# A new written-out order for a fused attention and mixer kernel, with other banks and tile shapes on TensorE

## The chip, the cores and the metric

The kernel runs on one core of one Trainium2 chip. The metric is the device time of one execution in microseconds (us). Before the change the median of three runs is 119.66 us (119.56 to 119.93). Beside the timed runs there is one profiled execution of 119.62 us, from which all rows of the trace come.

## The reference: what is computed

There are 8 batch items and 8 heads, with 576 rows of 64 elements each. Attention is taken twice. First 32 packed queries `p` attend to `k` and `v`. Then the 576 queries `q` attend to the 32 packed results. The result, 576 x 512 per item, goes through a token mixer with a ReLU and through an output projection.

```python
p_packed = sm_attn(p, k, v)                  # softmax over 576 keys
x = sm_attn(q, p_packed, p_packed)           # softmax over the 32 packed rows
wq, wk = x @ w_q, x @ w_k                    # 576 x 64 each, per item
W_tok = scale * (wq @ wk.T)                  # 576 x 576
out = relu(W_tok @ x) @ w_out                # 576 x 512
```

## The kernel before: tiles, engines and an order written by hand

There is no loop over items in the usual sense. A string named SCHEDULE (from line 10 on) lists every operation of all 8 items, each once, and line 742 calls them in that order. Each engine executes its own instructions in exactly the order in which the list names them; an instruction that has to wait holds up everything behind it on its engine. An entry has the form name@item, then the engine that executes it (v is VectorE or DVE, s is ScalarE or ACT, g is GpSimd or POOL), or, for TensorE (PE), the PSUM bank and a letter for the tile shape.

The operations of one item, in the order of its data:

- LK, LQ, LV load the keys, queries and values. POOL issues these loads on one queue, in the order of the list. Item 0's keys come by another way: in fp32 through SyncE (k_f, line 185), are cast by cA and cB, transposed by kf0 to kf3 and copied out of PSUM by kfe0 to kfe3. LP, tp, lp, tr and lq bring the packed queries into pT_bd.
- kt0 to kt2 and qt0 to qt2 transpose keys and queries on PE (line 306); ke and qe copy the result out of PSUM (lines 162 on ACT and 168 on DVE).
- s0 (line 327) multiplies the packed queries with the keys, nm (line 337, DVE) takes the row maximum, ex (line 343, ACT) the exponential, xt (line 155) transposes it, xe copies it out.
- pv (line 401) multiplies with the values. In an "E" form (line 391) it uses smaller tiles and 72 instead of 36 instructions. pp (line 418, DVE) scales, pt and pte transpose and copy out.
- et and em (lines 454 and 471) are the scores of the queries against the packed rows; mx, sb, x, sm, rr, ml (lines 483 to 527) are their softmax, on DVE, ACT and POOL. In items 0 and 7 it is cut into two parts. at and ae transpose and copy the result, a2T.
- pq, wk, wl, wq, g, y (lines 439 to 646) are the two projections and the mixer's inner products, with copies out pqe, wke, wqe, ge, ye. The mixer's own multiplication is m0, m1 and, for two items at once, m2 (lines 663 and 687), followed by the ReLU r.
- o0 to o4 (line 706) are the output projections, oe copies them out, st and sc store.
- u is a multiplication of zeros whose result nothing reads (line 213). It fills PE at the start.

PE's array is used in several tile shapes. Most operations exist with 128 x 64 tiles, two instructions side by side for the two halves of the output, and with letter A in the full 128 x 128 shape, with half as many instructions. pv and y use 64 x 64 tiles; m0 and m1 use 64 x 64, or with letter C 64 x 128.

Of the kernel before, what the change touches and what calls it, by code (L numbers as in the profile page):

```python
# [7 lines left out]


SCHEDULE = """  # L10
    LK@1 LP@0 LQ@0 cA1@0s u@0:0 u@0:0 u@0:0 u@0:0 u@0:0 u@0:0 u@0:0 u@0:0 u@0:0 tp@0:3 cA0@0s
# [1 line left out]
    kfe3@0s cw3@0 kfe0@0s u@0:1 u@0:1 u@0:1 s0@0:4 nm0@0 nm1@0 u@0:1 u@0:1 u@0:1 kt1@1:0 kt0@1:3
    ex0@0 ke1@1v cw2@0 kt2@1:1 ke0@1v ex1@0 tr@0:27 ke2@1s cw1@0 xt0@0:4A lq1@0v rc1@0 lq0@0v
    mk@0 u@0:0 u@0:0 u@0:0 u@0:0 u@0:0 qt0@0:5 xt1@0:1 qt2@0:3 cw0@0 xe1@0v qe2@0s xe0@0v s0@1:0
    qt1@0:6 nm0@1 u@0:7 u@0:7 pv@0:3 qe0@0v ex1@1 LK@3 pp0@0 qe1@0v ex0@1 u@0:7 u@0:7 pt@0:3
    pte@0v u@0:7 et@0:3 em@0 mx0@0 kt1@2:6 rc1@1 xt1@1:7 sb0@0 LQ@2 xt0@1:0A xe1@1s mx1@0
    kt0@2:1 x0@0 kt2@2:7 mk@1 sb1@0 ke2@2s ke0@2s ke1@2v x1@0 u@0:2 u@0:2 u@0:2 qt1@1:3 sm0@0v
    s0@2:4 qe1@1s rr0@0v xe0@1v ml0@0g sm1@0v u@0:2 u@0:2 qt2@1:0 qt0@1:2 qe2@1s nm0@2 LV@2
    at0@0:3A ae0@0s pv@1:0 rr1@0v ex0@2 pp0@1 ml2@0g qe0@1v u@0:7 u@0:7 pt@1:3A ml1@0g pq@0:0  # L20
    pte@1s ex1@2 et@1:1 em@1:A wo1@0 pqe@0s at1@0:4A mx0@1 xt0@2:0A wo0@0 ae1@0s pq@1:5 wk@0:7A
    wl@0 rc1@2 wq@0:4 sb0@1 wke@0s kt1@3:6 pqe@1s wkx@0g xt1@2:7A g@0:5A wqe@0v mk@2 x0@1
    kt2@3:1 ge@0v LK@4 kt0@3:2 y@0:3 xe0@2s sm0@1v qt2@2:5 LQ@3 ye@0s ke2@3s m0@0:34C ke0@3s
    LV@3 m1@0:01C r01@0s qt1@2:2 rr0@1v r00@0s xe1@2v ml1@1g ke1@3v qt0@2:7 qe2@2v qe0@2s pv@2:3
    ml2@1g r10@0v ml0@1g s0@3:5 pp0@2 r11@0s pt@2:3A qe1@2s nm0@3 at1@1:4A LQ@4 at0@1:0A pte@2s
    ae1@1s et@2:1 em@2:A ae0@1s LK@5 wk@1:0A ex0@3 mx0@2 wl@1 LV@4 o1@0:4 wke@1s ex1@3 o3@0:0
    wkx@1g sb0@2 LQ@5 g@1:5A pq@2:7 LK@7 ge@1s xt0@3:6 oe1@0v oe3@0s kt2@4:1 x0@2 kt1@4:5 LK@6
    ke2@4v kt0@4:0 o0@0:4 ke1@4s sm0@2v ke0@4s xt1@3:5 pqe@2s wq@1:2 y@1:0 rc1@3 wqe@1s qt2@3:7
    rr0@2v xe1@3v qt1@3:3 oe0@0s ml2@2g ye@1v qt0@3:2 ml1@2g qe1@3s qe2@3v m0@1:01C xe0@3s
    s0@4:3 r01@1s mk@3 m2@1:6 qe0@3s nm0@4 o2@0:7 r00@1s ml0@2g r2@1s pv@3:0 LV@5 ex1@4 o4@1:6A  # L30
    pp0@3 oe2@0v ex0@4 LQ@6 at0@2:0A pt@3:2A st1@0 at1@2:7A ae0@2s pte@3v m1@1:34C st0@0 ae1@2v
    et@3:0 r11@1s em@3:A oe4@1v r10@1s wk@2:7A rc1@4 mx0@3 xt1@4:5A xt0@4:6A xe1@4s qt2@4:3 wl@2
    qt0@4:5 wke@2s sb0@3 wq@2:4 qe2@4s wkx@2g o2@1:7 mk@4 x0@3 kt1@5:0 LV@6 kt2@5:1 ke1@5v
    qt1@4:2 qe0@4s pq@3:3 sm0@3v o3@1:0A wqe@2s qe1@4s g@2:4A ke2@5s xe0@4v o0@1:2A ge@2s pqe@3s
    rr0@3v oe3@1s ml1@3g y@2:3 oe0@1v pv@4:5 ye@2s m0@2:34 pp0@4 ml0@3g m1@2:20 r00@2s oe2@1v
    kt0@5:1 pt@4:5 r10@2s o1@1:6 r01@2v LQ@7 pte@4s r11@2s et@4:3 ml2@3g ke0@5s at0@3:7A em@4:A
    LV@7 ae0@3s o0@2:1A mx0@4 qt2@5:2 at1@3:7 qe2@5s sb0@4 o3@2:0 oe0@2s qt0@5:2 qt1@5:1 ae1@3v
    qe0@5s s0@5:3 oe1@1v x0@4 wk@3:2 qe1@5v wq@3:7 st0@1 nm0@5 kt2@7:6 st1@1 wqe@3s wl@3 o1@2:1
    ke2@7s wke@3v ex1@5 kt0@7:6 sm0@4v o2@2:7 wkx@3g ex0@5 kt0@6:2 oe3@2s g@3:3A rr0@4v oe1@2s
    xt1@5:4A ke0@6v ml2@4g xt0@5:5A ge@3s rc1@5 xe1@5v ml1@4g pq@4:2 kt1@6:1 pqe@4s y@3:3 xe0@5s  # L40
    ke1@6v kt2@6:2 ye@3s ml0@4g oe2@2s at1@4:5A ke2@6v m0@3:34C ke0@7s s0@6:0 ae1@4s mk@5 r01@3s
    pv@5:5 nm0@6 r00@3s at0@4:7A o1@3:3A ae0@4s pp0@5 ex0@6 wk@4:7A pt@5:5A ex1@6 m1@3:64C
    pte@5v wl@4 kt1@7:5 r11@3s wke@4v et@5:0 em@5:A oe1@3s rc1@6 wkx@4g o0@3:7A r10@3s mx0@5
    mk@6 ke1@7s g@4:4A qt0@6:5 sb0@5 wq@4:6 qe0@6s qt1@6:3 ge@4s wqe@4s o2@3:5 qe1@6s oe0@3v
    x0@5 s0@7:0 oe2@3v st0@3 m2@3:7A nm0@7 xt1@6:4A st0@2 r2@3s xt0@6:5A sm0@5g st2@1 o3@3:3A
    xe1@6s xe0@6s st1@2 ex0@7 y@4:4 pv@6:6 ye@4v ex1@7 pq@5:4 pp0@6 qt2@6:5 oe3@3s m1@4:67C
    m0@4:01C pqe@5s r10@4v xt1@7:2 st1@3 qe2@6s pt@6:3 o4@3:4 rr0@5v pte@6s r00@4s r11@4v ml0@5g
    r01@4s qt2@7:3 rc1@7 et@6:5 oe4@3s em@6:A ml1@5g xe1@7s o0@4:0A st2@3 qe2@7s mx0@6 ml2@5g
    xt0@7:2A at1@5:4A mk@7 at0@5:3A xe0@7v ae1@5s o1@4:1A sb0@6 ae0@5s oe0@4s wk@5:3A wl@5
    qt1@7:0 oe1@4v wke@5s pq@6:4 qt0@7:2 x0@6 qe1@7v wkx@5g st0@4 pv@7:5E pqe@6v wq@5:0 pp0@7  # L50
    qe0@7s sm0@6v g@5:4A wqe@5s pt@7:5A o2@4:3A pte@7s ge@5s rr0@6v et@7:0 y@5:4 em@7:A ml0@6g
    ye@5s oe2@4s mx0@7 m1@5:45 o3@4:6A r11@5s mx1@7 ml1@6g r10@5s sb0@7 at0@6:3A m2@5:7A ml2@6g
    ae0@6s o3@5:4A sb1@7 x0@7 r2@5s at1@6:3A x1@7 m0@5:20 o2@5:5 ae1@6s sm1@7v r01@5s wk@6:3
    wl@6 r00@5v o4@5:7 wke@6s rr1@7v oe3@5s sm0@7v wkx@6g wq@6:1 oe3@4s g@6:4 rr0@7v wqe@6s
    ml1@7v pq@7:3 ml0@7g st1@4 o0@5:0 ge@6s oe4@5s oe2@5s y@6:1 ml2@7g st2@5 at0@7:6 ye@6v
    pqe@7s at1@7:7 st1@5 oe0@5v ae0@7s m0@6:31 ae1@7s m1@6:25 r00@6s o1@5:4 r11@6v r10@6s wk@7:7
    oe1@5v wl@7 wq@7:0 wke@7s o2@6:2 r01@6s st0@5 wqe@7v wkx@7g g@7:1 o3@6:4 ge@7s oe2@6s y@7:6
    oe3@6v o1@6:2A ye@7s st1@6 m1@7:36 m0@7:47 r10@7v o0@6:1 r01@7s r11@7v r00@7s o3@7:0 oe1@6s
# [715 lines left out]
```

## Time and profile before

| What | Before |
|---|---|
| median of the runs | 119.66 us |
| profiled execution | 119.62 us |
| its span in the trace | 117.8 us |
| PE busy | 107.5 us, 2090 matrix instructions |
| DVE busy | 85.2 us |
| ACT busy | 83.6 us |
| POOL busy | 56.6 us |
| DMA moved | 25.47 MB, mean 216 GB/s |

A trace starts with the first instruction, so the profiled execution's 119.62 us are 1.82 us more than its span. Busy time of an engine is the time in which at least one instruction of it runs. On PE a busy share says only that instructions follow each other closely; the start of one to the start of the next tells what an operation costs. The chain of waits follows the last instruction back to whatever released it.

### The profile page before, as it was taken

Reading aid. Unit: us, or ns where it says so; the run is one execution under the profiler, and the core shown is the slowest. Engines: PE = TensorE matmul, PEld = TensorE weight load, DVE = VectorE, ACT = ScalarE, POOL = GpSimd, SP = SyncE. Lnnn points to the kernel's source line nnn. Section 1 sums busy time; section 2 is a strip of 40 time slices with the busy share of each in tenths; the row PEclk is TensorE's granted clock in tenths of the full one; section 3 lists DMA queues with packets and bytes.
Section 4 is the critical chain, followed back from the end, with each engine's and each line's share of the span. In section 5 each row is a group of like instructions: output and inputs, shape, how many; then the busy total and the mean of one; then the engine's idle time right before and its main releaser. Section 6 shows DMA issues by size and latency. Waiting matters only on the chain.

```text
span 117.8 us, 4809 instructions
## 1 busy us (share of the span) xinstructions
PE 107.5 (91%) x2090; PEld 72.0 (61%) x2100; DVE 85.2 (72%) x142; ACT 83.6 (71%) x188; POOL 56.6 (48%) x82
## 2 busy tenths in 40 slices
...
GB/s 53 354 217 203 208 209 207 207 188 208 208 206 207 209 207 210 206 210 282 304 205 212 203 261 319 212 207 243 385 387 97 172 0 6 288 242 182 209 365 147
DMA packets 18069, 25.47 MB, mean 216 GB/s; under 512 B 2304, under 2 KB 14592, under 8 KB 18048
## 3 DMA queue, kind: packets, MB, share of 16 engines
...
q14 instruction: 5, 0.04, 0.1%
...
## 4 chain that ended last, share of the span: by engine, by line
PE 58%; DVE 19%; ACT 7%; DMA 5%; issue 4%; POOL 3%; SPq 0%; DVEq 0%; ACTq 0%; POOLq 0%
PE psum L706 20%; PE psum L306 7%; PE psum L155 6%; DMA k_f<-in_k_dram 5%; DVE nmax L337 5%; DVE mx L483 4%; DVE rs L501 3%; POOL a L527 3%; PE psum L471 3%; PE psum L663 3%; ACT e1T L343 3%; PE psum L327 3%; DVE e L487 3%; PE psum L401 2%; ACT e L495 2%
## 5 line engine op out<-in xcount | busy, mean ns | idle before, releaser
L706 PE MATMUL psum<-w_out,reluT 128*64 128x512 bf16 (+1 forms) x199 | 31.6, 380 | 0.6
L527 POOL TENSOR_TENSOR a<-e,rr 128x512 bf16<-128x512 f32 (+1 forms) x23 | 18.7, 832 | 13.4 <-DVE rr L516 8.6
L706 PEld LDWEIGHTS <-reluT 128*64 128x64 bf16 (+1 forms) x208 | 12.5, 107 | 9.0 <-issue 0.8
L597 POOL TENSOR_TENSOR wkx<-wk,hmask 128x256 bf16<-128x256 bf16 x8 | 5.3, 668 | 23.1 <-ACT wk L162 13.7
L162 ACT ACTIVATE reluT<-psum 128x512 bf16<-128x512 f32 x24 | 13.7, 612 | 2.2 <-PE psum L663 2.1
L343 ACT ACTIVATE e1T<-psum,nmax 128x576 bf16<-128x576 f32 x16 | 11.7, 737 | 4.9 <-DVE nmax L337 4.7
L483 DVE TENSOR_REDUCE mx<-psum 128x36 f32<-128x1152 f32 (+2 forms) x10 | 11.1, 1116 | 5.1 <-PE psum L471 4.6
L337 DVE TENSOR_REDUCE nmax<-psum 128x2 f32<-128x1152 f32 (+1 forms) x9 | 10.9, 1219 | 4.2 <-PE psum L327 4.2
L306 PE MATMUL psum<-ident,q_sb 128*64 128x128 bf16 x288 | 12.3, 221 | 0.8 <-DMA q_sb<-in_q_dram 0.5
L162 ACT ACTIVATE qT<-psum 128x384 f32<-128x384 f32 x17 | 8.5, 497 | 6.3 <-PE psum L306 6.3
L162 ACT ACTIVATE o_sb<-psum 128x512 f32<-128x512 f32 x20 | 11.8, 604 | 0.8 <-PE psum L706 0.5
L213 PE MATMUL psum<-blank 128*64 128x512 bf16 x32 | 11.0, 469 | 1.2 <-DVE blank L193 1.2
L306 PEld LDWEIGHTS <-q_sb 128*64 128x64 bf16 x288 | 9.8, 110 | 3.6 <-issue 1.3
L501 DVE TENSOR_REDUCE rs<-e 128x36 f32<-128x1152 f32 (+2 forms) x9 | 9.7, 1074 | 2.1 <-ACT e L495 2.0
L487 DVE TENSOR_TENSOR e<-psum,mx 128x1152 f32<-128x1152 f32 (+2 forms) x10 | 11.1, 1114 | 0.2
L495 ACT ACTIVATE e<-e 128x1152 f32<-128x1152 f32 (+2 forms) x10 | 9.7, 971 | 1.8 <-DVE e L487 1.7
L306 PE MATMUL psum<-ident,k_sb 128*64 128x128 bf16 x252 | 10.2, 220 | 0.0
L168 DVE COPY o_sb<-psum 128x512 f32<-128x512 f32 x12 | 8.2, 684 | 1.9 <-PE psum L706 1.9
L306 PEld LDWEIGHTS <-k_sb 128*64 128x64 bf16 x252 | 8.4, 110 | 1.8 <-issue 0.6
L162 ACT ACTIVATE kT<-psum 128x384 f32<-128x384 f32 (+2 forms) x16 | 7.2, 478 | 0.9 <-PE psum L262 0.7
...
L155 PE MATMUL psum<-ident,e1T 128*128 128x128 bf16 (+1 forms) x93 | 6.3, 220 | 0.6 <-ACT e1T L343 0.6
...
## 6 DMA issues: line engine op xcount, KB each, us to landing
...
```

The lines of the kernel that those rows point to most:

```text
L155: nc.tensor.transpose(dst[r], src[:, r], ident)
L162: nc.scalar.activation(dst, src, func, scale=scale)
L213: nc.tensor.matmul(bank(ks[0], [n])[0:64], blank[:, 0:64], blank[:, 0:n], start=True, stop=True)
L306: nc.tensor.transpose(ps[64 * g2:64 * g2 + 64, 2 * gp:2 * gp + 2, jj, :], S_[b][src][:, gp + 2 * g2, j], ident,)
L337: nc.vector.tensor_reduce(tile("nmax", [P, 2], fp32, b)[:, h], S_[b]["s1"][:, h], axis=AX, op=MAX, negate=True)
L343: nc.scalar.activation(tile("e1T", [P, NJ, 2, 64], bf16, b)[:, :, h2], S_[b]["s1"][:, h2].rearrange("a (j s) -> a j s", s=64), EXP, bias=S ...
L483: nc.vector.tensor_reduce(tile("mx", [P, NU, 1], fp32, b)[:, r], S_[b]["e"][:, r], axis=AX, op=MAX)
L487: nc.vector.tensor_tensor(tile("e2", [P, NU, L], fp32, b)[:, r], S_[b]["e"][:, r], S_[b]["mx"][:, r].to_broadcast((P, r.stop - r.start, L) ...
L495: nc.scalar.activation(e, e, EXP, scale=scale)
L501: nc.vector.tensor_reduce(dst, src, axis=AX, op=ADD)
L527: (nc.vector if on == "v" else nc.gpsimd).tensor_tensor(tile("a2", [P, NU, L], bf16, b)[:, r], S_[b]["e2"][:, r], S_[b]["rr"][:, r].to_bro ...
L706: nc.tensor.matmul(ps[r], src[:, h2, gp, o + r.start:o + r.stop], w_out[:, 2 * gp + h2, :], start=(h2 + gp == 0), stop=(h2 + gp == 2),)
```

## The change

Only the string SCHEDULE changes; the functions that carry out the entries, the buffers and the numbers of their copies stay. Both lists hold the same operations, but for u: 38 instead of 32.

- The order on every engine is another one, and 185 operations of PE write to another bank of PSUM.
- 42 operations that copy out of PSUM, cast or take a ReLU go from ACT to DVE and 37 from DVE to ACT. ml2 of item 0 and sm0 of item 5 go from POOL to DVE, ml1 of item 7 from DVE to POOL.
- 15 operations of PE take the 128 x 128 shape that had 128 x 64 tiles, 17 the other way; seven of m0 and m1 go to the 64 x 128 shape and three leave it; pv of item 7 leaves the "E" form. PE's instructions go from 2100 to 2063.

Counted along both lists, PE goes from one tile shape to another 85 times before and 77 times after. From pv of item 2 to the end it is 61 and 53 times, and on that stretch both lists hold the same operations.

The first lines of the diff, and its last:

```diff
-    LK@1 LP@0 LQ@0 cA1@0s u@0:0 u@0:0 u@0:0 u@0:0 u@0:0 u@0:0 u@0:0 u@0:0 u@0:0 tp@0:3 cA0@0s
-    LV@0 kf1@0:5 kf0@0:0 LK@2 kfe1@0s cB0@0v cB1@0s lp@0v LQ@1 kf2@0:5 kf3@0:3 LV@1 kfe2@0s
...
-    oe0@7s sc0@7 oe4@7s st2@7
+    LP@0 LQ@0 LK@1 cA1@0v u@0:0 u@0:0 u@0:0 u@0:0 u@0:0 u@0:0 u@0:0 u@0:0 u@0:0 u@0:0 kf1@0:2
+    LV@0 LK@2 cB1@0s cB0@0v cA0@0v LQ@1 u@0:0 u@0:0 u@0:0 u@0:0 u@0:0 kf3@0:0 kf2@0:3 LV@1
+    kfe3@0s kfe1@0s tp@0:1 kfe2@0v cw3@0 kf0@0:4 lp@0s kfe0@0v cw1@0 u@0:5 u@0:5 s0@0:2 nm0@0
...
+    st2@7
```

The changed file is one line longer, so a line of it after the list has a number higher by one.

The first place is DVE between the row maximum of item 2 (nm0, the first row) and the first softmax of item 1 (mx0, the last row). Before:

```order
L337 TENSOR_REDUCE nmax<-psum 128x2
L516 RECIPROCAL rr<-rs 128x20
L418 TENSOR_TENSOR pp<-psum,mk 128x256
L168 COPY qT<-psum 128x4x96
L483 TENSOR_REDUCE mx<-psum 128x36
```

And in the changed list:

```order
L338 TENSOR_REDUCE nmax<-psum 128x2
L517 RECIPROCAL rr<-rs 128x20
L169 COPY qT<-psum 128x4x96
L419 TENSOR_TENSOR pp<-psum,mk 128x256
L528 TENSOR_TENSOR a_551<-e_448,rr 128x128
L169 COPY ppT<-psum 128x128
L169 COPY a2T<-psum 128x2x128
L169 CAST pqk<-psum 128x256
L484 TENSOR_REDUCE mx<-psum 128x36
```

The copy of transposed queries (qe2 of item 1) now stands ahead of pp of item 1 where qe0 stood behind it, and four operations (ml2 of item 0, pte of item 1, ae0 and pqe of item 0), which POOL and ACT carried out before, stand between pp and mx0.

The second place is PE from pv of item 7 to et of item 7. Of each operation one matrix instruction is shown, its loads of weights and its repetitions are left out. The rows tell the shape: an output of 32, 64 or 128 partitions. Before:

```order
L391 MATMUL psum<-v_sb,e_2205 32x64
L607 MATMUL psum<-a2T,pqk 64x512
L624 MATMUL psum<-wk,a_2165 128x64
L155 MATMUL psum<-ident,pp 128x128
L706 MATMUL psum<-w_out,reluT_2134 128x512
L454 MATMUL psum<-ppT,qT 64x64
```

And in the changed list:

```order
L402 MATMUL psum<-v_sb,e_2198 64x128
L307 MATMUL psum<-ident,q_sb 64x2x64
L588 MATMUL psum<-pqk,a2T 64x64
L156 MATMUL psum<-ident,pp 64x128
L608 MATMUL psum<-a2T,pqk 64x512
L440 MATMUL psum<-wqk,ppT 64x128
L625 MATMUL psum<-wk,a_2152 64x64
L707 MATMUL psum<-w_out,reluT_2154 64x512
L455 MATMUL psum<-ppT,qT 64x64
```

Before, the shape changes behind pv, ahead of g (line 624) and ahead of et (line 454). In the changed list it changes only once, behind pv; pt, g and the projection between them now have 128 x 64 tiles like their neighbours.

More of the change, by code (lines that the diff above doesn't have):

```diff
@@ L10 @@
 SCHEDULE = """
-    LK@1 LP@0 LQ@0 cA1@0s u@0:0 u@0:0 u@0:0 u@0:0 u@0:0 u@0:0 u@0:0 u@0:0 u@0:0 tp@0:3 cA0@0s
-    LV@0 kf1@0:5 kf0@0:0 LK@2 kfe1@0s cB0@0v cB1@0s lp@0v LQ@1 kf2@0:5 kf3@0:3 LV@1 kfe2@0s
[L13 to L58, printed above, removed]
@@ L59 @@
-    oe0@6v o1@7:2 st0@6 oe3@7s m2@7:1 sc3@7 oe1@7s o2@7:0 r2@7s sc1@7 o0@7:2 oe2@7s o4@7:0 sc2@7
-    oe0@7s sc0@7 oe4@7s st2@7
+    LP@0 LQ@0 LK@1 cA1@0v u@0:0 u@0:0 u@0:0 u@0:0 u@0:0 u@0:0 u@0:0 u@0:0 u@0:0 u@0:0 kf1@0:2
+    LV@0 LK@2 cB1@0s cB0@0v cA0@0v LQ@1 u@0:0 u@0:0 u@0:0 u@0:0 u@0:0 kf3@0:0 kf2@0:3 LV@1
+    kfe3@0s kfe1@0s tp@0:1 kfe2@0v cw3@0 kf0@0:4 lp@0s kfe0@0v cw1@0 u@0:5 u@0:5 s0@0:2 nm0@0
+    tr@0:10 nm1@0 ex0@0 u@0:5 u@0:5 qt0@0:5 qt1@0:6 ex1@0 qe0@0v qt2@0:7 lq1@0v qe2@0s xt0@0:2A
@@ new lines @@
+    xt1@0:4 rc1@0 xe1@0v lq0@0s mk@0 u@0:5 u@0:5 kt1@1:7 cw0@0 kt2@1:3 ke1@1v kt0@1:0 cw2@0
+    ke2@1s ke0@1v xe0@0s qe1@0s u@0:5 u@0:5 s0@1:3 nm0@1 u@0:1 pv@0:0 LK@3 pp0@0 ex1@1 u@0:7
+    u@0:7 u@0:7 pt@0:0 pte@0v ex0@1 u@0:7 et@0:0 em@0:A mx0@0 kt1@2:3 kt2@2:5 sb0@0 ke1@2s LQ@2
+    kt0@2:7 mx1@0 xt1@1:6A ke0@2s x0@0 sb1@0 ke2@2s sm0@0v x1@0 u@0:4 u@0:4 u@0:4 u@0:4 s0@2:0
+    rc1@1 qt2@1:5 xe1@1s LV@2 sm1@0v qt0@1:7 qt1@1:3 rr0@0v mk@1 xt0@1:4 nm0@2 qe1@1s ml0@0g
+    xe0@1s rr1@0v u@0:6 u@0:6 u@0:6 pv@1:3 ex0@2 qe2@1v ml1@0g pp0@1 qe0@1s pq@0:5 ml2@0v ex1@2
@@ new lines @@
+    pt@1:3A wo1@0 at0@0:7A pte@1v at1@0:4A ae0@0v wo0@0 et@1:0 ae1@0s pqe@0v em@1:A LK@4
+    xt0@2:3A mx0@1 xt1@2:4A wq@0:5 LQ@3 wk@0:6 kt2@3:7 xe1@2v LV@3 wl@0 sb0@1 wke@0s wqe@0s
+    u@0:4 u@0:4 kt0@3:6 wkx@0g xe0@2s pq@1:5 rc1@2 x0@1 LQ@4 g@0:0A kt1@3:3 ge@0v ke0@3v qt1@2:1
+    mk@2 ke1@3s qt2@2:2 sm0@1v ke2@3s y@0:3 ye@0s pqe@1s u@0:0 m1@0:34C qe2@2s rr0@1v qt0@2:7
+    r10@0v ml0@1g m0@0:50 qe0@2s qe1@2v r11@0s pv@2:6 ml1@1g r01@0s s0@3:1 pp0@2 r00@0s pt@2:6
+    ml2@1g nm0@3 at0@1:0A pte@2s at1@1:7A LK@5 ae0@1s et@2:4 ae1@1s em@2:A LV@4 wk@1:7A ex0@3
@@ new lines @@
+    mx0@2 wl@1 o1@0:0 LK@7 wke@1s ex1@3 wkx@1g o3@0:7 sb0@2 LQ@5 xt1@3:1 oe3@0s wq@1:2 kt0@4:3
+    x0@2 wqe@1v g@1:4 LK@6 kt2@4:5 ke0@4v xt0@3:2A oe1@0s ge@1v o0@0:7A rc1@3 sm0@2v xe0@3s mk@3
+    xe1@3s y@1:2 oe0@0s kt1@4:0 rr0@2v qt0@3:4 ye@1s ke2@4v ke1@4s pq@2:1 ml2@2g m0@1:23C qe0@3s
+    pqe@2v ml0@2g qt1@3:0 r00@1v qt2@3:1 qe1@3s s0@4:5 qe2@3s ml1@2g m2@1:0 r01@1s nm0@4 o2@0:4
+    r2@1s LV@5 m1@1:23C oe2@0v pv@3:0 ex0@4 LQ@6 o4@1:4A st1@0 pp0@3 r10@1s st0@0 r11@1s
+    at1@2:0A ex1@4 pt@3:1A at0@2:2A pte@3v qt1@4:3 ae1@2s LV@6 rc1@4 qt0@4:1 oe4@1s pq@3:0
@@ new lines @@
+    et@3:5 qe0@4v ae0@2s em@3:A mk@4 qe1@4s o2@1:2A pqe@3s mx0@3 wk@2:4A xt1@4:0A qt2@4:3 xe1@4s
+    sb0@3 kt1@5:1 qe2@4s kt2@5:0 ke1@5s wl@2 xt0@4:3 wke@2v wq@2:1 x0@3 oe2@1v o3@1:4A wkx@2g
+    ke2@5v xe0@4s LV@7 wqe@2s g@2:2A sm0@3v o0@1:0A ge@2s y@2:1 pv@4:6 rr0@3v ye@2s oe3@1s
+    ml2@3g m0@2:12C pp0@4 m1@2:35C ml1@3g oe0@1s r00@2v kt0@5:4 pt@4:6 o1@1:7 r01@2v pte@4s
+    ml0@3g r10@2s ke0@5v r11@2s et@4:0 at1@3:6A LQ@7 em@4:A ae1@3s at0@3:3A mx0@4 o3@2:6A ae0@3s
+    wk@3:3A oe3@2s wl@3 sb0@4 kt0@7:5 o0@2:4 ke0@7s oe1@1s kt2@7:6 wke@3v x0@4 s0@5:0 st0@1
@@ new lines @@
+    oe0@2v wkx@3g qt1@5:3 st1@1 nm0@5 qt0@5:7 ke2@7s g@3:4 qe1@5s o1@2:5 ge@3s sm0@4v ex0@5
+    qt2@5:4 o2@2:3 ex1@5 rr0@4v oe1@2s wq@3:6 ml2@4g pq@4:0 qe2@5s kt1@6:1 ml0@4g wqe@3v qe0@5s
+    kt0@6:5 ke1@6s rc1@5 kt2@6:2 pqe@4s ml1@4g y@3:6 ke2@6v at0@4:1A ye@3s xt0@5:0A ke0@6v
+    oe2@2s xt1@5:2A mk@5 xe0@5v m0@3:67C xe1@5s s0@6:3 ae0@4v r00@3s at1@4:1 r01@3s nm0@6
+    m1@3:20C ae1@4s pv@5:6 r10@3s o1@3:1A pp0@5 ex1@6 r11@3v wk@4:6A ex0@6 pt@5:7A kt1@7:0
+    pte@5v wl@4 rc1@6 et@5:2 ke1@7v em@5:A wke@4s oe1@3s xt1@6:7A wkx@4g mx0@5 xt0@6:5A o0@3:6A
```

16 lines of the change are left out of this document (added).

## Prediction

> **What bounds the kernel now.** I read the page first, then the busy time in stretches, then the chain of waits, and last the timelines of PE and DVE around the places that the change touches.
>
> ```profile
> span 117.8 us, 4809 instructions
> PE 107.5 (91%) x2090; PEld 72.0 (61%) x2100; DVE 85.2 (72%) x142; ACT 83.6 (71%) x188; POOL 56.6 (48%) x82
> ```
>
> A share of 91% is a mean over stages. The view by stretches (columns: length, then busy time of PE, weight loads, DVE, ACT and POOL, the granted clock, DMA share, GB/s) tells them apart. I cut it where pv of item 2 starts (36.35) and where PE ends (113.65):
>
> ```profile
> 17.50:27.00 9.50, 8.37 (x219) 5.81 (x219) 8.84 (x17) 5.35 (x12) 3.80 (x5) 1.00 1.32 202
> 27.00:36.35 9.35, 8.07 (x159) 5.60 (x159) 7.71 (x15) 7.31 (x18) 7.39 (x11) 1.00 1.22 208
> 36.35:64.00 27.65, 27.36 (x582) 19.02 (x587) 22.42 (x32) 21.85 (x51) 16.75 (x23) 1.00 1.20 226
> 64.00:92.00 28.00, 27.49 (x619) 20.05 (x621) 23.23 (x37) 24.68 (x59) 11.77 (x17) 1.00 1.05 260
> 92.00:113.65 21.65, 21.29 (x324) 12.33 (x324) 12.28 (x21) 16.80 (x37) 5.48 (x7) 1.00 0.43 167
> 113.65:117.80 4.15, 0.01 (x1) 0.00 (x0) 0.00 (x0) 0.60 (x1) 0.00 (x0) 1.00 0.54 204
> ```
>
> From 36.35 to 113.65 PE is idle for 0.29 + 0.51 + 0.36 = 1.16 us of 77.3. This is the stream: its length is the sum of what PE executes. Behind it stand 4.15 us in which the last tile is copied and stored. Ahead of it PE has idle time and fillers, and there DVE is at 8.84 of 9.50 us. What ends this head, the chain of waits and the waits of 30 to 40 us tell:
>
> ```profile
> 35.83 0.50 ACT qT L162
> 36.35 0.70 PE psum L401 x36
> PEld L401 <- DMA v_sb<-in_v_dram: 0.7, 1, 0.7
> ```
>
> The stream's first operation, pv of item 2, waited for a copy on ACT that ended at 36.33, and the load of its weights waited for the values of item 2 by DMA. Two conditions end here nearly together. So the time is head 36.35, stream 77.3, end 4.15, and 1.82 us outside the span.
>
> **The stream: fewer changes of tile shape.** The two lists hold the same operations from pv of item 2 on; the shape changes 61 times before and 53 times in the changed list. What a change costs is seen where the same 12 transposes stand once behind a 128 x 128 operation and once not (chain of waits):
>
> ```profile
> 51.95 0.50 PE psum L155 x9
> 52.45 0.46 PE psum L306 x12
> 52.90 0.12 PE psum L587 x8
> 53.03 0.34 PE psum L306 x12
> ```
>
> 0.46 behind L155 in the full shape, 0.34 behind L587 in the same shape as itself: 0.12 for one change. Elsewhere it is a little less: the next rows show o4 of item 1, full shape, behind pv; from 48.97 to 49.94 it takes 0.97 us, where eight instructions in the neighbours' shape take 0.86.
>
> ```profile
> 48.97 0.16 issue
> 49.13 0.81 PE psum L706 x3
> 49.94 0.69 PE psum L155 x11
> 63.17 1.03 PE L706 MATMUL psum<-w_out,reluT 128*64 128x512 bf16 x8
> 64.03 0.84 PE L306 MATMUL psum<-ident,q_sb 128*64 128x128 bf16 x24
> ```
>
> (The last two are of PE's timeline: 64.03 - 63.17 = 0.86 from start to start.) I take 0.11: 8 x 0.11 = **-0.88**, ends -0.80 and -0.96. The shape itself I cost at nothing: 0.97 less one change is 0.86 again, so the 15 operations that get the full shape and the 17 that lose it cost what they did. Nothing hides this gain, since the stream has only 1.16 us of idle time.
>
> pv of item 7 leaves its small tiles:
>
> ```profile
> 72.61 0.63 PE psum L401 x36
> 90.02 0.68 PE psum L391 x72
> ```
>
> 0.63 for 0.68: **-0.05**.
>
> **The stream: waits.** 42 copies go from ACT to DVE and 37 back. With a mean of some 0.5 us for a copy the stretch from 36.35 on loses some 2.5 us on ACT (63.3 busy in the three rows) and gains some 3 us on DVE (57.9 busy), sm0 of item 5 among it. Both stay below 64 of 77.3 us; this evens them out and costs nothing where PE does not wait. The tightest place is item 7, where the last softmax is followed by a wait of PE:
>
> ```profile
> 92.92 0.64 PE L471 MATMUL psum<-ppT,qT 128*128 128x64 bf16 x16
> 99.85 1.73 POOL L527 TENSOR_TENSOR a<-e,rr 128x512 bf16<-128x512 f32 x2 [0.32 <-DVE rr L516]
> 101.27 0.69 PE L155 MATMUL psum<-ident,a 128*64 128x128 bf16 x18 [0.25 <-POOL a L527]
> ```
>
> From em (92.92) to at (101.27) pass 8.35 us; PE had work for 8.1 of them. In the changed list it has some 7.9 us of work there, and the softmax runs on DVE, ACT and POOL in a slightly shorter order (sb0 stands ahead of mx1, so the exponentials start earlier). The wait stays about what it is. For all waits of the stream I take **0**; the ends are half of the 1.16 us gone (-0.6) and as much again as the largest single stretch shows, nearly twice 0.51 (+0.9).
>
> Loads: the bytes and nearly the order of the queue stay. The stretches from 17.5 to 64 show 202 to 226 GB/s, so the queue never stops. Packed queries and item 0's queries now go ahead of item 1's keys; the values of item 0 and of item 2 have the same bytes ahead of them and arrive when they did: nothing.
>
> **The head.** Two things move in it. First, PE's start:
>
> ```profile
> 1.18 4.05 PE L213 MATMUL psum<-blank 128*64 128x512 bf16 x9 [1.18 <-DVE blank L193]
> 7.76 1.17 PE L262 MATMUL psum<-ident,k_sb 128*64 128x128 bf16 x18 [0.19 <-DVE k_sb L168]
> 8.72 1.25 PE L213 MATMUL psum<-blank 128*64 128x512 bf16 x3
> 9.74 0.73 PE L327 MATMUL psum<-kT,pT_bd 128*64 128x512 bf16 x8
> 13.98 0.83 PE L213 MATMUL psum<-blank 128*64 128x512 bf16 x3
> ```
>
> Early fillers take 4.05 / 9 = 0.45 us each, later ones at most 0.83 / 3 = 0.28, although the page's clock row reads full speed. In the changed list five of them stand between kf1 and kf3, some 2.2 us, and the transposes of the second half, which could start at 7.76, wait for them until about 8.9. s0 of item 0 then starts some 1 us later than 9.74. Most of this is made up: up to the row maximum of item 2 DVE has three copies fewer (qe1 of item 0, ke1 of item 2, xe0 of item 1, some 1.3 us), so I expect that maximum within 0.1 us of where it was.
>
> Second, what follows that maximum on DVE (timeline, and three rows of the chain with the step of a copy of each size):
>
> ```profile
> 25.68 1.35 DVE L337 TENSOR_REDUCE nmax<-psum 128x2 f32<-128x1152 f32 x1
> 27.13 0.42 DVE L418 TENSOR_TENSOR pp<-psum,mk 128x256 bf16<-128x256 f32 x1
> 27.46 0.55 DVE L168 COPY qT<-psum 128x384 f32<-128x384 f32 x1
> 29.19 1.36 DVE L483 TENSOR_REDUCE mx<-psum 128x36 f32<-128x1152 f32 x1 [1.17 <-PE psum L471]
> 19.06 0.46 DVE qT L168
> 19.52 0.24 DVE ppT L168
> 24.70 0.34 DVE e L168
> 90.36 0.41 DVE L168 CAST pqk<-psum 128x256 bf16<-128x256 f32 x1
> 33.62 0.87 ACT L162 ACTIVATE kT<-psum 128x384 f32<-128x384 f32 x2
> ```
>
> Before, pp of item 1 ran at once, the copy of qT behind it was free because DVE then idled 1.17 us for PE. Now the copy stands ahead: pp is 0.46 later. Behind pp come ml2, pte, ae0, pqe; pte is the one that PE waits for, and the two transposes at0 and at1 of item 0 now stand on PE ahead of et, about 0.5 us, of which 0.3 is new ahead of mx. So mx of item 1 starts about 0.1 + 0.46 + 0.3 = 0.9 late. Before the stream's start ACT then has, behind item 1's exponential, six copies of about 0.87 / 2 = 0.4 us (ke1, ke2, ye, pqe, qe2, qe0), of which the last frees pv's bank. This puts pv of item 2 up to 0.95 us late. The other end is 0: the values of item 2 by DMA did not allow an earlier pv, and DVE's shorter list could make the delay up. Between them I take **+0.45**, the middle, since the two rows on which it depends (1.17 us of idle time that was there, and a tie at 36.33) speak for one each.
>
> One rule bears on the fillers. The Trainium skill, TensorE: Matmul & The Clock Gate, Part 1, says that PE's array starts at half clock, and goes to full clock after a window of about 3.4 us, free-running, in which it was busy. Ten fillers in a row instead of nine would then make it a little likelier that such a window ends by 5.5 us. The rows agree that the start is slow, but they show no opening after nine. By the rule the five fillers would be short and the sum without the head's loss.
>
> **Sum.** 119.62 - 0.88 - 0.05 + 0 + 0.45 = 119.14, so **119.1 us**. The profiled execution is 0.04 below the median of the runs, which changes nothing.
>
> **Rivals.** (1) The head loses nothing: pv of item 2 stays tied to its DMA, and a quarter of the idle time goes too: 119.62 - 0.93 - 0.3 = 118.4. For it: DVE's three copies less; against it: four operations put on DVE's chain. (2) The fillers are fast from 5.5 us on, the five between the transposes cost 0.28 instead of 0.45, and the head loses nothing: 119.62 - 0.93 = 118.7. Against it: nine fillers did not bring it. (3) No change: the stream gets shorter and PE runs into the softmax of each item sooner; 8.35 us from em to at were not enough before. Then the saved 0.9 comes back as waits in front of at or wk: 119.6. (4) Slower: all that DVE gets ahead of mx of item 1 lies on the path. qT 0.46, pqk 0.41, a2T 0.34 (by e's row of about that size), ppT 0.24, and for ml2, which has no row on DVE, an estimate of 0.3 between the last two, make 1.75, and it decides as soon as mx of item 1 starts after about 30.9 instead of 29.19: 119.62 - 0.93 + 1.75 = 120.4.
>
> **How the numbers follow.** Forecast 33% (its own range 118.7 to 119.4), (1) 22%, (2) 5%, (3) 20%, (4) 20%. The range 118.0 to 120.4 takes in the rivals and the ends of the sum: down 119.62 - 0.96 - 0.05 - 0.6 = 118.0; up to the fourth case. A measurement of this kernel can tell about 0.3% (0.36 us) from no change. Faster by more: (1), (2) and four fifths of the forecast, 53%. Within it: most of (3) and the rest of the forecast, 25%. Slower: (4) and a little of (3), 22%.
>
> **What would show it.** The changed profile should have pv of item 2 at about 36.8 us, and from there to PE's end some 76.4 us instead of 77.3, with idle time of PE near 1.2. The steps behind 128 x 128 operations should still show 0.1 us more. s0 of item 0 should start near 10.7, the row maximum of item 2 near 25.8, mx of item 1 near 30.1. I am wrong if pv of item 2 starts after 37.3, if PE idles more than 2 us in the stream (then look at at and wk of items 5 to 7), or if the stream shrinks by less than 0.5 although the shape changes eight times less.

## The result and the profile after

The changed kernel took 118.94 us (median of 20 runs, 118.16 to 120.63) beside 119.75 us of before (20 runs): a ratio of 0.9928, with a 95% interval of 0.9911 to 0.9946. Its profiled execution took 119.10 us. In a second comparison (e12 below) the same kernel took 119.46 us beside 119.51: 0.9990 (0.9969 to 1.0011). The ratios leave out single runs more than 1.5% above the fastest of their kernel (the profiled runs of e5 and e8 below are such runs, by their late heads), while the medians take all runs. By the medians the gain is 0.8 us in one comparison and 0.05 us in the other, and why it is not the same each time is part of what follows. The page of the changed kernel begins:

```profile
span 117.3 us, 4737 instructions
PE 105.5 (90%) x2054; PEld 70.7 (60%) x2063; DVE 88.1 (75%) x146; ACT 82.9 (71%) x185; POOL 53.9 (46%) x77
```

By stretches (PE alone: length, busy time and instructions, granted clock, DMA share, GB/s), cut at pv of item 2, at pv of item 5 and at PE's end:

```profile
36.12:73.38 37.26, 36.04 (x765) 1.00 1.19 234
73.38:113.13 39.75, 39.41 (x720) 1.00 0.70 214
113.13:117.30 4.17, 0.00 (x0) 0.91 0.54 201
```

The head is 0.23 us shorter than before (36.12 for 36.35). The stream is 77.01 us for 77.31, only 0.30 shorter. The end is as it was. What PE waits for has become transfers (chain of waits, its DMA pieces; then one row of the view of waits, and two of PE's timeline):

```profile
7.53 15.80 DMA q_sb<-in_q_dram
23.61 12.46 DMA v_sb<-in_v_dram
47.67 25.66 DMA v_sb<-in_v_dram
```

```profile
PE psum L402 <- DMA v_sb<-in_v_dram: 2.3, 5, 0.6
```

```profile
36.12 0.70 PE L402 MATMUL psum<-v_sb,e 64*64 64x128 bf16 x36 [0.30 <-DMA v_sb<-in_v_dram]
73.38 0.70 PE L402 MATMUL psum<-v_sb,e 64*64 64x128 bf16 x36 [0.60 <-DMA v_sb<-in_v_dram]
```

Here 23.61 + 12.46 = 36.07 is the landing of item 2's values, which ends the head, and 47.67 + 25.66 = 73.33 that of item 5's, for which pv of item 5 waits. Before, item 5's values had landed at 69.69 (records of the transfers) and pv of item 5 started at 72.55.

PE and DVE in the head, the places of the prediction:

```profile
1.19 3.69 PE L214 MATMUL psum<-blank 128*64 128x512 bf16 x10 [1.19 <-DVE blank L194]
5.93 1.24 PE L214 MATMUL psum<-blank 128*64 128x512 bf16 x5
7.42 0.69 PE L263 MATMUL psum<-ident,k_sb 128*64 128x128 bf16 x18 [0.24 <-ACT k_sb L163]
9.36 0.68 PE L328 MATMUL psum<-kT,pT_bd 128*64 128x512 bf16 x8 [0.16 <-DVE kT L169]
```

```profile
24.86 1.29 DVE L338 TENSOR_REDUCE nmax<-psum 128x2 f32<-128x1152 f32 x1
27.07 0.43 DVE L419 TENSOR_TENSOR pp<-psum,mk 128x256 bf16<-128x256 f32 x1 [0.33 <-PE psum L402]
29.31 1.36 DVE L484 TENSOR_REDUCE mx<-psum 128x36 f32<-128x1152 f32 x1 [0.28 <-PE psum L472]
```

The five fillers took 0.25 us each, and the transposes behind them waited for a cast on ACT, not for them. s0 of item 0 starts at 9.36 (before 9.74), the row maximum of item 2 at 24.86 (25.68), mx of item 1 at 29.31 (29.19).

### The profile page after: what moved, and what is told of

Same layout as the page of the kernel before. It is cut to its first block, busy times and chain, and to the rows that moved or that the text cites. A ratio compares the mean times of both kernels' runs of the same rounds, so it can differ in the third digit from the quotient of the medians.

```text
span 117.3 us, 4737 instructions
## 1 busy us (share of the span) xinstructions
PE 105.5 (90%) x2054; PEld 70.7 (60%) x2063; DVE 88.1 (75%) x146; ACT 82.9 (71%) x185; POOL 53.9 (46%) x77
## 4 chain that ended last, share of the span: by engine, by line
DMA 46%; PE 39%; POOL 8%; DVE 3%; issue 1%; ACT 1%; POOLq 0%; DVEq 0%
DMA v_sb<-in_v_dram 32%; PE psum L707 19%; DMA q_sb<-in_q_dram 13%; PE psum L156 4%; PE psum L307 2%; PE psum L402 2%; POOL a L528 2%; PE psum L664 2%; PE psum L608 2%; PE psum L472 2%; POOL pT_bd L199 1%; POOL k_sb L173 1%; PE psum L572 1%; POOL p_b L234 1%; DVE rs L502 1%
## 5 line engine op out<-in xcount | busy, mean ns | idle before, releaser
L163 ACT ACTIVATE o_sb<-psum 128x512 f32<-128x512 f32 x23 | 13.5, 598 | 4.1 <-PE psum L707 4.1
L214 PE MATMUL psum<-blank 128*64 128x512 bf16 x38 | 11.7, 424 | 1.3 <-DVE blank L194 1.2
L502 DVE TENSOR_REDUCE rs<-e 128x36 f32<-128x1152 f32 (+2 forms) x10 | 11.0, 1101 | 0.3 <-ACT e L496 0.2
L165 DVE TENSOR_SCALAR reluT<-psum 128x512 bf16<-128x512 f32 x14 | 9.2, 678 | 2.6 <-PE psum L664 2.6
L307 PE MATMUL psum<-ident,q_sb 128*64 128x128 bf16 x288 | 11.1, 220 | 0.0
L163 ACT ACTIVATE reluT<-psum 128x512 bf16<-128x512 f32 x18 | 10.1, 601 | 0.2
L307 PEld LDWEIGHTS <-q_sb 128*64 128x64 bf16 x288 | 9.2, 110 | 1.4 <-issue 0.4
L163 ACT ACTIVATE kT<-psum 128x384 f32<-128x384 f32 (+1 forms) x13 | 5.9, 472 | 2.6 <-PE psum L307 2.1
L173 POOL DMA_DIRECT2D v_sb<-in_v_dram x8 | 6.1, 763 | 3.4 <-DMA q_sb<-in_q_dram 2.3
L402 PE MATMUL psum<-v_sb,e 64*64 64x128 bf16 x288 | 5.6, 218 | 2.3 <-DMA v_sb<-in_v_dram 2.3
```

The lines of the kernel that those rows point to most:

```text
L163: nc.scalar.activation(dst, src, func, scale=scale)
L165: nc.vector.tensor_scalar(dst, src, 0.0, None, op0=MAX)
L214: nc.tensor.matmul(bank(ks[0], [n])[0:64], blank[:, 0:64], blank[:, 0:n], start=True, stop=True)
L307: nc.tensor.transpose(ps[64 * g2:64 * g2 + 64, 2 * gp:2 * gp + 2, jj, :], S_[b][src][:, gp + 2 * g2, j], ident,)
L502: nc.vector.tensor_reduce(dst, src, axis=AX, op=ADD)
```

## The experiments

The runs asked four things: what the letters (tile shapes) are worth, why PE stops in some of them, what pv of item 5 waits for, and what ends the head.

### The letters alone

e1 keeps before's list and takes from 37 operations of the stream their wide shape, so that the shape changes 40 times instead of 61. e3 does the same to the changed list (42 operations, 35 changes instead of 53). e2 gives the changed list the shapes that before had (37 operations, 70 changes). Order, banks and engines stay.

```diff
-    pt@2:3A at1@1:4A at0@1:0A em@2:A wk@1:0A
+    pt@2:3 at1@1:4 at0@1:0 em@2: wk@1:0
```

> The list before with its order, banks and engines untouched; from pv of item 2 on only the tile shapes of 37 PE operations are changed (all to 128 x 64), so that PE changes its shape 40 times there instead of 61. Theory A (a change of shape costs about 0.11 us wherever PE does not wait): 21 x 0.11 = 2.3 us less, 0.4 us back because em takes 0.51 instead of 0.44 us in the narrow shape in four items and up to 0.5 us back where pv of item 4 meets its values by DMA: 117.8 to 118.3 us. Theory B (the shape is worth nothing, what the order gains is gained elsewhere): 119.5 to 120.0 us.

> The changed list with its order, banks and engines; from pv of item 2 on the 37 PE operations whose shape differs between the lists get the shape that they had before (pv of item 7 excepted). Now the shape changes 70 times instead of 53: 9 more ahead of pv of item 5 and 8 more behind it. Theory A with a bound by DMA (pv of item 5 waited 0.60 us for its values, pv of item 4 0.27): 17 x 0.11 = 1.9 us more, of which up to 0.87 is absorbed by those waits: 119.9 to 120.8 us. Theory A without that bound: 120.8 us. Theory B: 118.9 us.

> The changed list; from pv of item 2 on 42 PE operations change their shape so that it changes 35 times instead of 53: 13 fewer ahead of pv of item 5, 5 fewer behind it. Theory A with the bound by DMA: pv of item 5 cannot start before its values land at 73.3 us, so only the 5 behind it count: 0.5 us less, about 118.4 us, and the waits of pv for DMA grow by more than 1 us. Theory A without that bound: 18 x 0.11 = 2.0 us less, 117.0 us. Theory B: 118.9 us.

Measured: e1 125.92 us, 1.0554 (1.0516 to 1.0593) of before. e3 128.34 us, 1.0753 (1.0690 to 1.0816). e2 120.68 us, 1.0117 (1.0071 to 1.0164). e2, with 17 changes more, lies in the range of theory A. But fewer changes made the kernel slower by 6 to 9 us, which neither theory had. In e1's timeline PE stops in the middle of operations, released by nothing that the profile knows; its view of waits has 2.5 + 2.5 + 2.2 = 7.2 us of this kind:

```profile
PE psum L398 <- issue: 2.5, 2, 1.9
PE psum L152 <- issue: 2.5, 3, 1.1
PE psum L303 <- issue: 2.2, 2, 1.6
```

```profile
59.96 0.64 PE L398 MATMUL psum<-v_sb,e 64*64 64x128 bf16 x32 [0.64 <-issue]
65.88 0.41 PE L303 MATMUL psum<-ident,q_sb 128*64 128x128 bf16 x8 [1.62 <-issue]
78.00 0.31 PE L398 MATMUL psum<-v_sb,e 64*64 64x128 bf16 x8 [1.86 <-issue]
```

In the last row pv of item 5 has only 8 of its 36 instructions left: it stopped in its midst. One DMA queue carries instructions; in e1 and in the changed kernel (packets, MB, share):

```profile
q8 instruction: 18, 0.29, 0.9%
```

```profile
q8 instruction: 16, 0.26, 0.9%
```

A packet is 16 KB. Put beside PE's instructions, weight loads counted too, its arrivals in e1 give this table, worked out from the records of the trace:

```
PE's instruction number at the stop   PE goes on at   16 KB landed at   remainder of the number by 256
1473                                  41.65           39.99             193
1984                                  53.49           52.18             192
2240                                  59.96           58.36             192
2496                                  65.88           64.43             192
3008                                  78.00           76.57             192
3263                                  83.92           82.65             191
4031                                  97.79           96.46             191
```

Every stop of 0.5 us or more in e1's stream stands in this table, at nearly the same remainder by 256 (a few records of PE are missing from a trace, so it slips by one or two), and ends 1.3 to 1.7 us after a block has landed. So 16 KB hold 256 instructions, and PE stops because the next block is not there. From 39 to 82 us the blocks come every 6.1 us. Before needs one every 6.1 us as well (its instruction 960 starts at 30.89 us, 2496 at 67.54: six blocks in 36.65 us) and has no stop of 0.5 us or more at this remainder. A narrow operation has twice the instructions of a wide one: e1 has 2348 matrix instructions for 2100.

### The same with few loads

e5 is e3, and e6 the changed kernel, both without the 15 loads of items 3 to 7.

```diff
+        if b > 2:
+            S_[b][name] = S_[2][name]
+            return
         t = tile(name, [P, 4, NJ, Dh], bf16, b)
```

> The run with 35 shape changes in the stream (after's order, 42 operations narrowed, 128.34 us), without the 15 loads of q, k and v of items 3 to 7: those items work on item 2's values, so their rows of the result are others. Instruction theory: TensorE stopped in that run because its instructions come in blocks of 16 KB over the DMA engines that the loads keep full, about 6.1 us for a block of 256. Without the loads a block comes in some 3.4 us, the stops after 40 us go, and the 18 changes fewer than in the changed kernel are worth 18 x 0.11 = 2.0 us: 115.3 to 116.0 us, under its pair with the same loads left out (e6). Rival, the narrow operations are slow by themselves: 126 to 128 us, far above its pair.

> The changed kernel, nothing else altered, without the 15 loads of q, k and v of items 3 to 7 (items 3 to 7 work on item 2's values): the pair of e5. Instruction theory: the changed kernel has no stops to lose; what goes is the waits for the values of items 4 and 5 and a little of the small waits, together 1.3 to 1.6 us of the 1.63 us that TensorE stands idle in the stream: 117.3 to 117.8 us. Rival, the loads slow TensorE as such: 115 to 116 us.

Measured: e5 119.29 us, 0.9917 (0.9870 to 0.9963); e6 118.99 us, 0.9945 (0.9926 to 0.9964). PE from pv of item 2 to 85 us, and from there to its end, for e3, e5 and e6:

```profile
36.59:85.00 48.41, 40.32 (x1070) 1.00 1.14 219
85.00:123.52 38.52, 37.59 (x695) 0.96 0.44 172
```

```profile
37.69:85.00 47.31, 46.87 (x1236) 1.00 0.13 48
85.00:114.36 29.36, 28.79 (x527) 1.00 0.57 225
```

```profile
36.63:85.00 48.37, 47.70 (x1033) 1.00 0.12 47
85.00:113.11 28.11, 27.89 (x468) 1.00 0.60 233
```

With the loads PE idles 8.09 us of the first 48.41, without them 0.44 of 47.31, with the same list. The stops up to 85 us are the loads' doing: this is shown. One stop of e5 is left behind that, at the same remainder by 256:

```profile
92.48 0.28 PE L625 MATMUL psum<-wk,a 128*64 128x64 bf16 x6 [0.41 <-issue]
```

But e5 misses its 115.3 to 116.0 us and does not beat its pair by what the theory wanted: its stream is 76.67 us, e6's 76.48, although the shape changes 18 times less. What the changes save is spent elsewhere (below). e6 misses its own 117.3 to 117.8 as well: its stream is 0.5 us shorter than the changed kernel's, its head 0.5 longer (36.63).

### The price of a change of shape

e9 adds 33 small fillers after pv of item 5, in the shape of their neighbours; e10 the same 33 in the 128 x 128 shape, 66 changes more. The list gets the same entries in both (z, ahead of an operation with 128 x 64 tiles, in its own bank); only the width differs:

```diff
-        nc.tensor.matmul(bank(ks[0], [64])[0:64], blank[:, 0:64], blank[:, 0:64], start=True, stop=True)
+        nc.tensor.matmul(bank(ks[0], [64])[0:128], blank[:, 0:128], blank[:, 0:64], start=True, stop=True)
```

> The changed kernel with 33 small fillers after pv of item 5 (64 columns each, the loads nearly over), each in the shape 128x64 between two operations that already have this shape, so that no shape change is added. All theories: 33 x 0.03 to 0.05 us = 1.0 to 1.6 us over the changed kernel: 120.0 to 120.7 us. It is the base for its pair with other shapes (e10).

> The same 33 fillers in the same places, with as many instructions, but in the shape 128x128: 66 shape changes more. Theory of the prediction, 0.11 us a change: 7.3 us over e9, 127 to 128 us. Theory that a change costs about half of that, as e5 against e6 (18 changes fewer, no gain) lets one think: 3 to 4 us over e9, 123 to 124.5 us. Rival, a change costs nothing and the gain of the changed kernel has another source: as e9.

Measured: e9 119.33 us, 0.9955 (0.9938 to 0.9973) of before, e10 127.22 us, 1.0633 (1.0599 to 1.0666) of before. From pv of item 5 to PE's end, e9 and then e10:

```profile
73.18:113.65 40.47, 40.47 (x759) 1.00 0.70 212
```

```profile
72.95:120.71 47.76, 47.76 (x757) 1.00 0.59 179
```

PE is never idle in either. 47.76 - 40.47 = 7.29 us for 66 changes: 0.110 us each, the prediction's price to the digit (by the medians, 7.89 / 66 = 0.12). e9 itself stayed below its 120.0 to 120.7: 33 fillers without a change are too cheap to stand out of the spread of the times.

Single rows agree. These are et of item 4 (L455), at1 of item 3, em of item 4 (L472) and at0 of item 3, first in e5, where all have 128 x 64 tiles, then in e6, where only et has:

```profile
62.26 0.23 PE L455 MATMUL psum<-ppT,qT 128*64 128x64 bf16 x4
62.31 0.45 PE L153 MATMUL psum<-ident,a 128*64 128x128 bf16 x10
62.60 0.67 PE L472 MATMUL psum<-ppT,qT 128*64 128x64 bf16 x32
63.10 0.39 PE L153 MATMUL psum<-ident,a 128*64 128x128 bf16 x8
```

```profile
61.25 0.23 PE L455 MATMUL psum<-ppT,qT 128*64 128x64 bf16 x4
61.41 0.45 PE L153 MATMUL psum<-ident,a 128*128 128x128 bf16 x5
61.70 0.63 PE L472 MATMUL psum<-ppT,qT 128*128 128x64 bf16 x16
62.16 0.39 PE L153 MATMUL psum<-ident,a 128*128 128x128 bf16 x4
```

From its start to the next one's, et takes 0.05 us ahead of its own shape and 0.16 ahead of the full one: 0.11 for the change. at1 takes 0.29 in both widths, em 0.50 instead of 0.46. (In other rows of the two runs wk and g take 0.25 instead of 0.23, an output projection 0.86 in both widths.)

So the 18 changes of e5 should be worth 2.0 us, and yet its stream is 0.2 longer than e6's. The stop of 0.41 accounts for a part. Some 1.8 us are left, 0.04 for each of the 42 narrowed operations if they were all to blame. The rows do not bear that out: by the steps of the trace, less 0.11 for each change, the narrowed operations take about 0.7 us more by themselves, half of it in the five em. The rest is spread over many small steps, and its cause is not shown. In e1 it is alike: its stream (35.49 to 119.86) is 7.06 us longer than before's, the stops less the changes give 7.2 - 21 x 0.11 = 4.9, and 2.2 us come on top.

### What pv of item 5 waits for

The two stores of item 1 (512 KB each) go out at 64.90 and 65.48 us, beside the load of item 5's values. e4 leaves them out (first diff); e8 sends them behind all loads (second).

```diff
-    sb0@4 kt0@7:5 o0@2:4 ke0@7s oe1@1s kt2@7:6 wke@3v x0@4 s0@5:0 st0@1
-    oe0@2v wkx@3g qt1@5:3 st1@1 nm0@5
+    sb0@4 kt0@7:5 o0@2:4 ke0@7s oe1@1s kt2@7:6 wke@3v x0@4 s0@5:0
+    oe0@2v wkx@3g qt1@5:3 nm0@5
```

```diff
-            nc.sync.dma_start(rows(b)[:, :, i], S_[b][f"o_sb{i}"])
+            (nc.gpsimd if b == 1 else nc.sync).dma_start(rows(b)[:, :, i], S_[b][f"o_sb{i}"])
-    g=2, y=4, reluT0=2, reluT1=2, reluX=2, o_sb0=2, o_sb1=2, ox=2, nmax=4, rsum=4, rrec=4, mk=3, mx=2, rs=2, rr=2,
+    g=2, y=4, reluT0=2, reluT1=2, reluX=2, o_sb0=3, o_sb1=3, ox=2, nmax=4, rsum=4, rrec=4, mk=2, mx=2, rs=2, rr=2,
```

> The changed list without the two 512 KB stores of item 1's output (these rows are left out of the result), which run beside the load of item 5's values. Theory of the bound by DMA: these values land some 3 us earlier than 73.3, pv of item 5 no longer waits, and the time falls by its 0.6 us, to about 118.3 us. Rival: another wait takes its place within an item (softmax or PSUM), 118.8 to 119.0 us.

> The changed kernel with the two large stores of item 1 sent on GpSimd's queue, where they stand behind all loads, instead of SyncE's; o_sb gets three buffers of each kind in place of two, mk two in place of three. Theory that the stores delay the load of item 5's values: it lands at 70.9 us as with the stores left out, pv of item 5 starts without a wait, and the stream from pv of item 2 to the end of TensorE is 76.4 us in place of 77.0: 118.3 us. Rival, that the stores' issue on GpSimd, or the buffers that they hold until 85 us and later, cost it elsewhere: 118.9 to 119.6 us.

Measured: e4 119.42 us, 0.9961 (0.9928 to 0.9994); e8 119.62 us, 0.9975 (0.9940 to 1.0009). The stream of e4, then of e8:

```profile
36.93:73.40 36.47, 36.06 (x763) 1.00 1.20 221
73.40:113.31 39.91, 39.57 (x722) 1.00 0.63 201
```

```profile
38.09:74.50 36.41, 36.00 (x764) 1.00 1.20 221
74.50:114.32 39.82, 39.48 (x722) 1.00 0.66 221
```

Item 5's values landed at 70.86 and 71.08, pv of item 5 did not wait, and the stream is 76.38 and 76.23 us, as expected. Ahead of them in the queue stand the keys of item 6. From the landing of these keys to that of item 5's values pass 2.81 and 2.83 us in e4 and e8, 5.52 in the changed kernel, and 3.5 to 5.6 in the six other profiles with the two stores at 64 to 67 us and all loads (e2, e7, e9 to e12). So the stores delay the load. But before has the same stores, at 65.61 and 66.20 us, and there the step is 2.78 and the next load, item 6's queries, takes 6.33: some tenths of a us decide which load the stores hit. Nor does the delay always reach PE: of these seven profiles pv of item 5 waits over 0.1 us for its values in two, the changed kernel's (0.60) and e10's (0.73). The second profile of the same kernel, e12, does not have this wait.

The time did not follow, because in the profiled runs pv of item 2 started at 36.93 and 38.09 us instead of 36.12. In e8 the chain of waits leaves no doubt of what ended the head:

```profile
24.28 13.76 DMA v_sb<-in_v_dram
38.04 0.04 issue
38.09 0.70 PE psum L399 x36
```

### What ends the head

e7 takes the five fillers ahead of kf3 away; e12 is the changed kernel again; e11 takes before's list up to pv of item 2 and the changed list from there.

```diff
-    LV@0 LK@2 cB1@0s cB0@0v cA0@0v LQ@1 u@0:0 u@0:0 u@0:0 u@0:0 u@0:0 kf3@0:0
+    LV@0 LK@2 cB1@0s cB0@0v cA0@0v LQ@1 kf3@0:0
```

> The changed kernel without the five fillers that stand ahead of kf3 of item 0. The prediction's head term: s0 of item 0 starts about 1 us earlier, and pv of item 2 0.45 us earlier: 35.7 us, 118.5 us in all. DMA theory: pv of item 2 starts when the values of item 2 have landed, within 0.1 us of it, wherever that is (36.1 to 36.9 us): no gain, 118.8 to 119.2 us.

> The changed kernel itself beside the other three. By the first comparison 0.9928 of before, 118.6 to 119.0 us. By the theory of the head: where the profiled run shows the keys of item 1 landing at 13.4 to 13.6 us, pv of item 2 starts at the landing of item 2's values near 36.1 us; where they land at 15.4 us or later, pv of item 2 starts at 36.6 us or later, and the run takes 0.5 us and more beyond the other.

> The list of before up to pv of item 2 and, from there, the changed kernel's (four steps of items 0 to 2 that before had still open, and one load, stand between). Theory from the profiles: pv of item 2 starts at the landing of item 2's values or 21.2 us after the landing of item 1's keys, whichever is later; with before's order of the first loads the keys land at 9.5 to 10.1 us and the values bind, at 35.4 to 36.4 us, in every run; the stream of the changed kernel takes 76.3 to 77.0 us, what follows 4.2, and 1.8 lie outside the span: 117.8 to 119.3 us, likeliest 118.5, and the single times lie as close as before's. Rival, the head costs nothing by itself and the changed kernel's gain needs its own head: 119.0 to 119.6 us.

Measured: e7 119.80 us, 1.0029 (1.0005 to 1.0053); s0 of item 0 starts at 9.23 instead of 9.36, and pv of item 2 at 37.25, 0.04 after its values landed. The prediction's head falls; the time is also beyond the 118.8 to 119.2 of the other theory, since the values landed later than it had allowed for. e12 took 119.46 us, beyond its 118.6 to 119.0, and has its pv of item 2 at 36.50, and its chain of waits runs over the keys of item 1:

```profile
5.13 10.18 DMA k_sb<-in_k_dram
15.31 0.04 issue
15.36 1.22 PE psum L307 x36
```

All profiles with the changed kernel's head (e7: but for five fillers), in us (landings by the records of the transfers; e5 and e6 without item 3's keys, so that item 2's values come early):

| Run | keys of item 1 land | + 21.19 | values of item 2 land | pv of item 2 starts |
|---|---|---|---|---|
| e10 | 13.47 | 34.66 | 35.92 | 35.97 |
| e2 | 13.43 | 34.62 | 36.00 | 36.04 |
| changed kernel | 13.61 | 34.80 | 36.08 | 36.12 |
| e12 (the same kernel) | 15.31 | 36.50 | 36.43 | 36.50 |
| e3 | 15.40 | 36.59 | 36.22 | 36.59 |
| e9 | 15.44 | 36.63 | 36.49 | 36.62 |
| e6 | 15.45 | 36.64 | 33.99 | 36.63 |
| e5 | 16.50 | 37.69 | 34.99 | 37.69 |
| e4 | 15.43 | 36.62 | 36.89 | 36.93 |
| e7 | 15.40 | 36.59 | 37.21 | 37.25 |
| e8 | 15.46 | 36.65 | 38.04 | 38.09 |

The start is the later of two times, within 0.05 us in all eleven: the landing of the values, or 21.19 us after the landing of the keys. With the same order of loads the keys land at 13.4 to 13.6 or at 15.3 us and later, and, with all loads, the values spread from 35.9 to 38.0. Both times of the keys occur in one comparison (e10 and e12). The fork lies one load earlier: the packed queries land by 7.8 to 8.1 us in all eleven, item 0's queries at 10.6 to 10.8 in the first three of the table and at 12.4 to 13.0 in the others. Where the keys come at 13.5 the head is shorter than in before's profile (36.35), where they come at 15.4 it is longer. This would carry the unequal gains; single timed runs have no trace, so for them it is not shown. Before's head has a spread of its own: e1, with the same list up to there, starts pv of item 2 at 35.49. In both profiles it starts 0.04 us after its values have landed.

In e11 item 1's keys stand first again and land at 9.24 us, the values of item 2 at 35.64, and pv of item 2 starts at 35.68. e11 took 118.23 us (117.94 to 118.39), 0.9893 (0.9879 to 0.9907) of before, in the same comparison in which the changed kernel had 0.9990. Its stream, and for e12 the same:

```profile
35.68:72.20 36.52, 36.35 (x768) 1.00 1.19 234
72.20:112.11 39.91, 39.87 (x726) 1.00 0.72 217
```

```profile
36.50:73.25 36.75, 36.48 (x777) 1.00 1.19 234
73.25:113.11 39.86, 39.83 (x726) 1.00 0.72 217
```

35.68 + 76.43 + 4.2 + 1.8 = 118.1, and its profiled execution took 118.08 us. e11 is faster than both kernels, and its times lie within 0.5 us of each other, where e12's spread over 1.6.

## Why the prediction was right in the sum and not in the steps

The forecast was 119.14 us; the profiled execution took 119.10. That they agree so closely is luck: two errors of the same size cancelled, and in e12, the same kernel, the time comes to the same 119.08 from other parts (head 36.50, stream 76.61).

- **Fewer changes, -0.88: right in size.** The price of 0.11 is measured (0.110), and where pv of item 5 does not wait the stream of the changed list takes 76.2 to 76.6 us (e4, e6, e7, e8, e11, e12) instead of 77.31, about the forecast 76.4. The changed kernel's first profile shows 77.01. Something else is in this fall: the 0.25 us that at of item 7 waited for POOL before is in none of these profiles.
- **Waits of the stream, 0: wrong by +0.6 in the profiled execution.** The step that failed is "arrive when they did: nothing". It looked at items 0 and 2 only. Item 5's values land 3.64 us later than before, 0.90 of it already with item 6's keys ahead of them and 2.74 in the step beside the two stores, and pv of item 5 waits (0.60 in the row above). The case named as "wrong if the stream shrinks by less than 0.5" came true (0.30); the place was not at or wk but pv, so rival (3) had the effect and not the cause. That the stores delay the load is shown by e4 and e8, whose streams are 0.6 to 0.8 shorter. The wait belongs to this execution rather than to the list, as e12 shows.
- **The head, +0.45: wrong in its mechanism.** In the profiled execution the head of rival (1) held: pv of item 2 is tied to its transfer, at 36.12. In the other ten profiles of this head the median start is 36.6, near the 36.8 that was forecast, but by the arrival of the keys and values, which the forecast held to be the same as before. Of the signs named, s0 of item 0 started at 9.36 and not near 10.7, the row maximum of item 2 at 24.86 and not near 25.8, mx of item 1 at 29.31 and not near 30.1. The five fillers took 0.25 us each and stood in time in which PE waited for a cast; without them s0 starts 0.13 earlier (e7). Before's profile hides a part of the delay that was forecast, because its clock record goes to full speed only at 9.61 us: e1 and e11, with before's list there and full speed from 5.17 and 4.60, have s0 at 8.77 and 8.73 and mx at 28.38 and 28.84. Beside these the changed head's s0 is 0.6 us late, 0.13 of it by the fillers.
- **"The shape itself I cost at nothing": wrong, without much weight here.** Narrowing costs nothing in some operations and 0.02 to 0.04 us in others by the rows above, some 1.8 us in all between e5 and e6 with what is not explained, and beside the loads the added instructions have to arrive. The change moves about as many operations one way as the other (PE's instructions go from 2100 to 2063), so the sum did not show it. It decides over e1 and e3, where my expectations went by the changes alone and were wrong by 8 to 11 us.
- **Rival (2), fast fillers.** Its premise came true: the clock record of the trace goes to full speed at 3.95 us instead of 9.61 (the page's clock row counts the time ahead of the first record as full speed), and ten fillers took 3.69 us where nine had taken 4.05. The tenth filler is not shown to be the cause: with nine the record has 4.60 in e11, and with ten it has up to 6.97 (e3). It was worth nothing, since the head waits for transfers. The full-speed stretches of the two profiles last 109.23 and 112.64 us, 32 and 33 times 3.413. The Trainium skill, TensorE: Matmul & The Clock Gate, Part 1, has a free-running window of that length; the trace agrees.
- **Rival (4)** did not occur: its point, mx of item 1 after 30.9, was not reached.

e2 stays partly open. Its 17 changes more should cost 1.9 us; the stream of its profile (36.04 to 113.36) is 77.32, about 0.9 longer than the 76.4 without a wait, and its single times (119.33 to 121.28) are spread by the head as well. Which of its 37 letters give the rest back wasn't tried. Nor was it found why the same first loads land at one of two times. In the three profiles with item 1's keys first (before, e1, e11) these land at 9.2 to 10.1 us and pv of item 2 starts with its values; that the order decides it fits this, but these kernels have another head altogether.
